# Attention into a feed-forward layer on one core: global heads on other PSUM banks, and a written order of three engines from step 18

## Chip, cores and metric

The kernel runs on one core of one Trainium2 chip. The time is in device microseconds of one execution. The profile is of one execution, taken on the chip.

## What is computed

The reference is cut to what matters. There are 8 batches of 8 heads, with 512 local and 32 global positions of width 64.

```python
k_all, v_all = concat([k_g, k_l], 2), concat([v_g, v_l], 2)
out_g = sm(scale * q_g @ k_all.T) @ v_all              # global queries see all
s_ll = where(abs(pos - pos.T) <= 32, scale * q_l @ k_l.T, -1e9)
out_l = sm(concat([scale * q_l @ k_g.T, s_ll])) @ v_all  # local: a window and the globals
x = concat([out_g, out_l], 2).transpose(0, 2, 1, 3).reshape(4352, 512)
h = relu(x @ w_in)                                     # 512 -> 2048
out = (s * h * h + b) @ w_out                          # 2048 -> 512
```

## The kernel before

**Steps.** One main loop runs over steps j. In steps 0 to 127 a step takes one head of one half of a batch (16 steps a batch: two halves of eight heads; batch b has steps 16b to 16b + 15). Steps 0 to 15 take heads in pairs. From step 10 on, each step also takes one eighth of a feed-forward tile of 256 tokens: with m = j − 10 (`LAG` is 10), `ffn_in(m)` makes 256 columns of the hidden layer, and `ffn_out(m − 1)` adds the part before to the output. There are 17 such tiles; the last holds the global rows.

**What a step does.** `scores(j)` has four matmuls into `ps_s` (L351), and between the first and the second of a block the product of the global queries with the same keys into `ps_g` (L363). DVE adds the mask and takes the minimum (L207), ACT exponentiates (L214), DVE normalizes (L223) and packs (L384), and a DMA transpose turns the weights (L386). One step later ACT copies them back (`join`, L394), and in odd steps `pv` multiplies a pair of heads with the values into `ps_op` (L318), which ACT copies into x (L325). The global product is read by ACT into `tg` (L371) and by DVE into `sg` (L372). `ffn_in` has 24 matmuls into `ps_h` (L493); ACT makes r (L501), DVE squares it (L502), ACT makes g (L509) and DVE its rest (L510). `ffn_out` has 12 matmuls into `acc` (L528). Numbers are split into a high and a low part of the type fp32r, so x is split as well (`x_split`, L464 on ACT and L465 on DVE, into `xs`), in steps 17, 25, 33 and so on. The split of the keys and queries (`kq`) runs on ACT (L191, L193) and on POOL (L192, L194).

**Global heads.** The rows `sg` of four heads fill up over a batch. Their softmax runs in steps 16b + 12 and 16b + 16 (`g_softmax`). Three steps later (16b + 15 and 16b + 19) `g_transposes` turns them on TensorE into a tile of blocks 0 to 3 and a tile of block 4 (both `ps_tg`, L417), ahead of the first and of the second half of `ffn_out`. ACT (L421) and DVE (L422) read each into `pg`. One and three steps after that `g_pv` multiplies `pg` with the split values `vsg` (L434 on ACT, L435 on POOL) into `ps_og` (L443), behind `ffn_in`. ACT (L447) and DVE (L448) read it, and a DMA stores the row.

**Banks.** The matmul results lie in eight PSUM banks, by tag: "s" (`ps_s`), "g", "t", "o", two of "h" (`ps_h`), "acc0" and "acc1". A tile of a tag waits until the tile before it in that bank has been read. "g" holds `ps_g`, `ps_og` and one tile of `ps_tg`; "t" holds the other tile of `ps_tg` and, up to step 15, the transposes of the first heads (`ps_t`); "o" holds `ps_op`.

**Order.** Up to step `ORDERED` the instructions of every engine are placed by a scheduler that weighs them by a model. From `ORDERED` on, TensorE, ACT and DVE take theirs in the order in which the program writes them; the queues of POOL and SP stay with the scheduler. In the step `ORDERED` itself the global product is made late, behind `ffn_in` (`late_scores`). All engines take their instructions strictly in order.

Of the kernel before, what the change touches and what calls it, by code (L numbers as in the profile page):

```python
# [10 lines left out]
F32 = mybir.dt.float32  # L11
# [10 lines left out]
P = 128  # L22
# [22 lines left out]
NF = 16  # L45
AHEAD = 0
LAG = 10
ORDERED = 25
WARM_FIRST = 28

SPARE = 12
# [11 lines left out]
def f32(ap):  # L63
    return ap.bitcast(F32)
# [3 lines left out]
def window_attention_then_ffn(ctx: ExitStack, tc: tile.TileContext, qd, qp, qg, kw, vw, vg, w_in, w_out, sv, bv, out):  # L68
# [5 lines left out]
    ps = ctx.enter_context(tc.tile_pool(name="ps", bufs=1, space=bass.MemoryType.PSUM))  # L74
# [266 lines left out]
    def scores(j):  # L341
        b, hf, h = slot(j)
        ks, qs = st_.pop(("ks", j)), st_.pop(("qs", j))
        p_s = ps.tile([P, 512], F32, tag="s", name=f"ps_s{j}")
        late = j == ORDERED
        if not late:
# [63 lines left out]
    def g_transposes(b, g):  # L410
        sg = st_["sg", b, g]
        pg = st_["pg", b, g] = sb.tile([P, 5, 4, 2, SG], F32R, tag="pg", name=f"pg{b}_{g}", bufs=1)
        for c0, c1, tag in ((0, 4, "g"), (4, 5, "t")) if b else ((4, 5, "g"), (0, 4, "t")):
            p_t = ps.tile([P, 4, P], F32, tag=tag, name=f"ps_tg{b}_{g}_{c0}")
            for c in range(c0, c1):
                s0 = min(c * P, SGW - P)
                nc.tensor.transpose(out=p_t[:, c - c0, :], in_=sg[:, s0:s0 + P], identity=ident)  # L417
            v = p_t[:, 0:c1 - c0].rearrange("p c (h q) -> p (c h) q", h=4)
            ph, pl = (pg[:, c0:c1, :, i, :].rearrange("p c h q -> p (c h) q") for i in range(2))
            with tc.high_priority():  # L420
                nc.scalar.copy(out=ph, in_=v)  # L421
                nc.vector.tensor_sub(out=pl, in0=v, in1=f32(ph))  # L422
            yield
# [13 lines left out]

    def g_pv(b, h):
        pg, vs = st_["pg", b, h // 4], st_.pop(("vsg", b, h))
        p_g = ps.tile([P, 512], F32, tag="g", name=f"ps_og{b}_{h}")  # L440
        for i in range(2):
            for c in range(5):
                nc.tensor.matmul(  # L443
                    p_g[0:64, i * P:(i + 1) * P], lhsT=pg[:, c, h % 4 + i], rhs=vs[:, i, c], start=(c == 0), stop=(c == 4),
                )
        t = sb.tile([32, 2 * P + 40], F32, tag="og", name=f"og{b}_{h}", bufs=1)[:, 0:2 * P]
        nc.scalar.copy(out=t, in_=p_g[32:64, 0:2 * P])  # L447
        nc.vector.tensor_add(out=t, in0=p_g[0:32, 0:2 * P], in1=t)  # L448
        xr = sb.tile([P, 264], F32, tag="xr", name=f"xr{b}_{h}", bufs=1)[0:32, 0:2 * D]
        t = t.rearrange("q (h a d) -> q h a d", h=2, a=2)  # L450
        nc.vector.tensor_add(out=xr.rearrange("q (h d) -> q h d", h=2), in0=t[:, :, 0], in1=t[:, :, 1])
        nc.sync.dma_start(xg_d[b * SG:(b + 1) * SG, h * D:(h + 2) * D], xr)
# [98 lines left out]
    for b in range(B):  # L551
        for g in range(2):
            s0 = 16 * b + G_AT[g]
            early[s0].append(lambda b=b, g=g: g_softmax(b, g))
            turns[s0 + G_TR] = g_transposes(b, g)
            for i in range(2):
                h = 4 * g + 2 * i
                early[s0 + G_TR + G_LD[i] - 1].append(lambda b=b, h=h: g_load(b, h))
                early[s0 + G_TR + G_LD[i]].append(lambda b=b, h=h: g_split(b, h))
                extra[s0 + G_TR + G_PV[i]].append(lambda b=b, h=h: g_pv(b, h))  # L560
# [21 lines left out]
    for j in range(NM + LAG + 2):  # L582
        if j == ORDERED:
            fixed.enter_context(tc.manual_schedule(engines=ENGINES))
# [32 lines left out]
        if 0 <= m < NM:  # L617
            t = m // 8 + 1
# [90 lines left out]
```

## Time and profile before

| | |
|---|---|
| median of 3 runs | 1042.64 us (1041.49 to 1045.37) |
| the profiled execution's own time | 1042.14 us |
| its span, first to last instruction | 1040.3 us |
| mean granted TensorE clock | 0.977 |
| TensorE matmul busy | 977.0 us (94%) |
| ScalarE (ACT) busy | 748.3 us (72%) |
| VectorE (DVE) busy | 691.8 us (66%) |
| GpSimd (POOL) busy | 273.1 us (26%) |

Busy time is the time in which an engine had an instruction running. A wait is the idle time of an engine ahead of an instruction, with the instruction on another engine that ended it. In a row of the timeline the first number is the start in us from the span's start, the second the duration, and what stands in square brackets is the wait; rows of equal instructions that follow each other are merged (x24). PE is TensorE, PEld its loading of weights.

### The profile page before, as it was taken

How to read it: one execution, taken by the hardware profiler on the slowest of the kernel's cores; microseconds unless marked ns; L12 is line 12 of the kernel's file. 1: busy time of each engine (PE TensorE's matmuls, PEld its weight loads, DVE VectorE, ACT ScalarE, POOL GpSimd, SP SyncE). 2: the span in 40 equal slices, each digit the busy share in tenths (PEclk: the TensorE clock that was granted, in tenths of full speed). 3: DMA queues.
4: the chain of work that ended last, by engine and by line, in shares of the span. 5: the costliest groups of instructions: out<-in, count | busy, mean ns of one | idle time of the engine just before them, and what ended most of it. 6: DMA issues, size and time to landing. Idle time of an engine off the chain costs nothing. (4 is left out here: it accounts for less than half of the span.)

```text
span 1040.3 us, 19938 instructions
## 1 busy us (share of the span) xinstructions
PE 977.0 (94%) x7060; PEld 862.5 (83%) x7060; DVE 691.8 (66%) x2092; ACT 748.3 (72%) x1618; POOL 273.1 (26%) x309
## 2 busy tenths in 40 slices
PE   5789998998999999998999999998999899999996
PEld 2468887887999889987999789987999789999895
DVE  6999667676667766776667766776667766653321
ACT  6987677778777777778778787777777787763221
POOL 0011322234323332234223342233323242221000
PEclk8679999999999999999999999999999999999998
DMA  9951444444444454444444454444444553321000
GB/s 327 350 176 61 99 115 100 109 105 121 107 108 99 100 123 116 109 102 121 117 108 98 103 129 103 109 106 125 103 115 96 104 131 91 87 62 35 11 21 20
DMA packets 179627, 115.07 MB, mean 111 GB/s; under 512 B 124744, under 2 KB 166728, under 8 KB 179528
## 3 DMA queue, kind: packets, MB, share of 16 engines
q1 hardware_dynamic: 179240, 112.76, 41.7%
q8 instruction: 55, 0.90, 0.4%
q10 hardware_dynamic: 288, 1.05, 0.4%
q14 instruction: 44, 0.36, 0.1%
HBM read 74.97 MB, written 9.44 MB: 81 GB/s over the span
## 5 line engine op out<-in xcount | busy, mean ns | idle before, releaser
L493 PE MATMUL ps_h<-xs,w 128*128 128x256 f32 x3264 | 421.1, 284 | 5.7 <-ACT xs L464 3.3
L493 PEld LDWEIGHTS ps_h<-xs,w 128*128 128x128 f32 x3264 | 399.0, 190 | 15.9 <-ACT xs L464 3.5
L528 PE MATMUL acc<-w,g 128*128 128x512 f32 x1632 | 404.2, 395 | 0.3 <-ACT g L509 0.2
L528 PEld LDWEIGHTS acc<-w,g 128*128 128x128 f32 x1632 | 294.8, 188 | 59.2 <-DVE g L510 1.1
L192 POOL TENSOR_TENSOR kq<-rk,kq 64x416 fp32r<-64x416 f32 x112 | 124.8, 1114 | 585.4 <-ACT kq L191 585.3
L509 ACT ACTIVATE g<-r,b_t 128x512 fp32r<-128x512 f32 x136 | 98.4, 724 | 123.0 <-DVE r L502 123.0
L510 DVE SCALAR_TENSOR_TENSOR g<-r,b_t,g 128x512 fp32r<-128x512 f32 x136 | 102.3, 752 | 99.8 <-ACT g L509 99.8
L394 ACT COPY ptp<-turned 128x1024 int16<-128x1024 int16 x112 | 152.7, 1363 | 6.2 <-DMA turned<-two 6.2
L502 DVE SCALAR_TENSOR_TENSOR r<-ps_h,s_t,r 128x512 f32<-128x512 f32 x136 | 101.3, 745 | 72.3 <-ACT r L501 70.6
L214 ACT ACTIVATE sm<-sm,nm 128x224 f32<-128x224 f32 (+1 forms) x256 | 117.8, 461 | 13.7 <-DVE nm L207 10.5
L501 ACT ACTIVATE r<-ps_h 128x512 f32<-128x512 f32 x136 | 81.4, 599 | 52.3 <-PE ps_h L493 49.5
L384 DVE COPY two<-sm 128x256 int16<-128x256 int16 x448 | 106.3, 300 | 0.1
L194 POOL TENSOR_TENSOR kq<-rq,kq 128x256 fp32r<-128x256 f32 x112 | 84.1, 751 | 8.8
L207 DVE CUSTOM_DVE_ANT_0 sm<-ps_s,mask 128x192 f32<-128x192 f32 (+1 forms) x224 | 74.4, 370 | 17.1 <-PE ps_s L351 16.8
L435 POOL TENSOR_TENSOR vsg<-rvg,vsg 128x320 fp32r<-128x320 f32 x64 | 55.7, 891 | 88.4 <-ACT vsg L434 88.4
L351 PE MATMUL ps_s<-kq 128*128 128x192 f32 (+1 forms) x448 | 78.7, 267 | 0.0
L351 PEld LDWEIGHTS ps_s<-kq 128*128 128x128 f32 x448 | 72.2, 191 | 7.4 <-issue 0.3
L223 DVE TENSOR_SCALAR sm<-sm,ss 128x192 f32<-128x192 f32 (+1 forms) x224 | 66.2, 337 | 3.9
L318 PE MATMUL ps_op<-ptp,rvp 128*64 128x128 f32 (+2 forms) x1024 | 67.8, 267 | 0.7 <-ACT ptp L310 0.6
L217 DVE TENSOR_SCALAR ss<-ss 128x2 f32<-128x2 f32 (+1 forms) x120 | 32.8, 273 | 51.4 <-ACT sm L214 51.2
L318 PEld LDWEIGHTS ps_op<-ptp,rvp 128*64 128x64 f32 x1024 | 53.6, 140 | 13.0 <-issue 2.7
L372 DVE TENSOR_TENSOR sg<-ps_g,tg 32x256 f32<-32x256 f32 (+1 forms) x112 | 48.2, 431 | 21.7 <-ACT tg L371 18.1
(68 smaller groups left out, 806.0 us busy)
## 6 DMA issues: line engine op xcount, KB each, us to landing
rvp<-in_vw SPq DMA_DIRECT2D x64, 256.0 KB, 2.8
rq<-in_qd SPq DMA_DIRECT2D x112, 128.0 KB, 2.3
rk<-in_kw SPq DMA_DIRECT2D x56, 208.0 KB, 2.5
rvg<-in_vg SPq DMA_DIRECT2D x32, 320.0 KB, 3.0
out<-o SPq DMA_DIRECT2D x34, 256.0 KB, 3.1
wst<-in_w_in SPq DMA_DIRECT2D x15, 512.0 KB, 6.3
wst<-in_w_out SPq DMA_DIRECT2D x15, 512.0 KB, 7.2
turned<-two SPq DMA_TRANSPOSE x112, 3.1
```

The costliest lines, as they stand in the source:

```text
L192: (nc.gpsimd if K_POOL(j) else nc.vector).tensor_sub(out=ks[p1:p1 + 64], in0=rk[p0:p0 + 64], in1=f32(ks[p0:p0 + 64]))
L194: nc.gpsimd.tensor_sub(out=qs[:, 1, :], in0=rq, in1=f32(qs[:, 0, :]))
L214: nc.scalar.activation(out=p, in_=p, func=AF.Exp, bias=nm[:, n:n + 1], scale=-1.0, accum_out=ss[:, n:n + 1],)
L318: nc.tensor.matmul(p_o[64 * k:64 * k + 64, 0, blk, q0:q0 + n], lhsT=rv[:, k, v:v + D], rhs=pt[:, k, o] if i < NF // 2 else pt[:, k, 2 * bl ...
L351: nc.tensor.matmul(p_s[:, cols], lhsT=qs[:, a, blk * P:(blk + 1) * P], rhs=ks[:, cols], start=(a == 0), stop=(a == 1),)
L384: nc.vector.tensor_copy(out=two[:, 2 * blk + c], in_=sm[:, :, c0:c0 + P])
L394: nc.scalar.copy(out=pt.bitcast(I16).rearrange("p c (q h) -> p c h q", h=2), in_=st_.pop(("turned", j)))
L493: nc.tensor.matmul(p_h[:, k], lhsT=wi[f][:, a, c, :], rhs=xs[:, e, c, :], start=(n == 0), stop=(n == 11),)
L502: nc.vector.scalar_tensor_tensor(out=r, in0=p_h, scalar=s_t, in1=r, op0=ALU.mult, op1=ALU.mult)
L509: nc.scalar.activation(out=g[:, 0], in_=r, func=AF.Identity, bias=b_t)
L510: nc.vector.scalar_tensor_tensor(out=g[:, 1], in0=r, scalar=b_t, in1=f32(g[:, 0]), op0=ALU.add, op1=ALU.subtract,)
L528: nc.tensor.matmul(oacc[t][i], lhsT=g[:, a, k, i * P:(i + 1) * P], rhs=wo[f][:, e, :], start=(pr == 0 and n == 0), stop=(pr == 7 and n == 5),)
```

## The change

The two tiles of `ps_tg` go to "t" (blocks 0 to 3) and "o" (block 4) in every batch, `ps_og` goes to "t", and the written order begins at step 18. "g" is left to `ps_g`.

```diff
-ORDERED = 25
+ORDERED = 18
...
     def g_transposes(b, g):
...
-        for c0, c1, tag in ((0, 4, "g"), (4, 5, "t")) if b else ((4, 5, "g"), (0, 4, "t")):
+        for c0, c1, tag in ((0, 4, "t"), (4, 5, "o")):
             p_t = ps.tile([P, 4, P], F32, tag=tag, name=f"ps_tg{b}_{g}_{c0}")
...
     def g_pv(b, h):
...
-        p_g = ps.tile([P, 512], F32, tag="g", name=f"ps_og{b}_{h}")
+        p_g = ps.tile([P, 512], F32, tag="t", name=f"ps_og{b}_{h}")
```

From step 27 on TensorE, ACT and DVE have the same instructions in the same order in both kernels; there only the banks differ. Steps 18 to 26 change their order, and the steps before them in places.

TensorE from the scores of step 18 on, before (the number behind a name is the step, the part of the feed-forward layer or the batch and head; the number at its end only tells buffers apart):

```order
L351 MATMUL ps_s18_1278<-kq18_1177 128x192 x2
L351 MATMUL ps_s18_1278<-kq18_1177 128x224 x2
L493 MATMUL ps_h8_1309<-xs1_1244,w0_152 128x256
L318 MATMUL ps_op8_1410<-ptp8_1212,rvp8_1066 64x128
L417 MATMUL ps_tg0_1_0_1472<-ident_66,sg4_335 128x128 x4
L493 MATMUL ps_h8_1309<-xs1_1244,w0_152 128x256 x11
L363 MATMUL ps_g17_1185<-kq17_1057,qgs1_981 64x256
L493 MATMUL ps_h8_1309<-xs1_1244,w1_195 128x256 x12
L528 MATMUL acc0_0_686<-w14_805,g7_1252 128x512 x3
L528 MATMUL acc0_0_686<-w15_817,g7_1252 128x512 x3
```

The same place with the change:

```order
L351 MATMUL ps_s18_1280<-kq18_1177 128x192 x2
L351 MATMUL ps_s18_1280<-kq18_1177 128x224 x2
L493 MATMUL ps_h8_1306<-xs1_1244,w0_152 128x256 x12
L493 MATMUL ps_h8_1306<-xs1_1244,w1_195 128x256 x12
L443 MATMUL ps_og0_2_1331<-vsg0_2_1214,pg0_0_1033 64x128 x10
L363 MATMUL ps_g18_1354<-kq18_1177,qgs1_981 64x256
L528 MATMUL acc0_0_686<-w14_805,g7_1252 128x512 x3
L528 MATMUL acc0_0_686<-w15_817,g7_1252 128x512 x3
L528 MATMUL acc0_1_687<-w14_805,g7_1252 128x512 x3
```

The transposes of the second four heads, a piece of `ps_op` and the global product of step 17 stood inside `ffn_in(8)` and have left it; the product of step 18 is the late one now, and `ps_og` of heads 2 and 3 stands ahead of it.

ACT from the exponentials of step 18 on, before:

```order
L214 ACTIVATE sm18_1287,ss18_1286<-sm18_1287,nm18_1285 128x192
L214 ACTIVATE sm18_1287,ss18_1286<-sm18_1287,nm18_1285 128x224
L371 COPY tg17_1196<-ps_g17_1185 32x256
L191 CAST kq20_1375<-rk20_1272 64x416
L193 CAST kq20_1375<-rq20_1274 128x256
L501 ACTIVATE r8_1351<-ps_h8_1309 128x512
L536 COPY o0_0_1369<-acc0_0_686 128x512
L509 ACTIVATE g8_1354<-r8_1351,b_t_72 128x512
L394 COPY ptp9_1421<-turned18_1304 128x4x2x128
L371 COPY tg18_1290<-ps_g18_1279 32x256
L191 CAST kq21_1485<-rk20_1272 64x416
L536 COPY o0_1_1372<-acc0_1_687 128x512
```

With the change:

```order
L214 ACTIVATE sm18_1287,ss18_1286<-sm18_1287,nm18_1285 128x192
L214 ACTIVATE sm18_1287,ss18_1286<-sm18_1287,nm18_1285 128x224
L394 COPY ptp8_1212<-turned17_1210 128x4x2x128
L447 COPY og0_2_1342<-ps_og0_2_1331 32x256
L501 ACTIVATE r8_1348<-ps_h8_1306 128x512
L509 ACTIVATE g8_1351<-r8_1348,b_t_72 128x512
L371 COPY tg18_1356<-ps_g18_1354 32x256
L536 COPY o0_0_1371<-acc0_0_686 128x512
L536 COPY o0_1_1374<-acc0_1_687 128x512
L191 CAST kq20_1377<-rk20_1274 64x416
L193 CAST kq20_1377<-rq20_1276 128x256
L371 COPY tg19_1396<-ps_g19_1385 32x256
```

The casts of the keys and queries of steps 20 and 21 stood between r, g and the stores of `acc` and now follow them; the copy of `ps_og` and r and g of part 8 have moved ahead of them.

## Rows read from the trace of the kernel before

**Rows 1.** Page, part 1: busy time of each engine, share of the span, instructions.

```profile
PE 977.0 (94%) x7060; PEld 862.5 (83%) x7060; DVE 691.8 (66%) x2092; ACT 748.3 (72%) x1618; POOL 273.1 (26%) x309
```

**Rows 2.** Who TensorE waits for, whole span: total us, times, longest us.

```profile
PE ps_g L363 <- DVE pg L422: 20.2, 12, 2.2
PE ps_og L443 <- DVE sg L372: 7.0, 7, 1.1
...
PE ps_h L493 <- DVE xs L465: 1.7, 6, 0.3
```

**Rows 3.** Windows from one step's first `ps_s` to the next: steps 48, 50-54, 60.

```profile
core 0: us, PE busy (x) PEld busy (x) DVE busy (x) ACT busy (x) POOL busy (x), PEclk, DMA share, GB/s
...
342.27:350.37 8.10, 6.93 (x53) 6.22 (x51) 5.95 (x22) 5.80 (x14) 1.81 (x2) 1.00 0.49 117
357.71:366.18 8.47, 7.23 (x52) 6.35 (x51) 7.03 (x20) 5.59 (x13) 2.28 (x3) 1.00 0.43 110
366.18:373.93 7.75, 7.75 (x64) 6.93 (x62) 4.30 (x16) 6.62 (x15) 3.13 (x4) 1.00 0.56 159
373.93:383.11 9.18, 6.99 (x52) 6.23 (x51) 5.90 (x21) 6.71 (x15) 2.20 (x3) 1.00 0.57 131
383.11:390.26 7.15, 7.15 (x59) 6.43 (x58) 4.76 (x16) 6.08 (x14) 3.60 (x4) 1.00 0.57 76
390.26:397.03 6.77, 6.77 (x52) 6.25 (x51) 4.60 (x18) 4.98 (x12) 1.81 (x2) 1.00 0.61 159
430.77:436.89 6.12, 6.12 (x42) 5.63 (x41) 4.38 (x16) 4.53 (x10) 1.83 (x2) 1.00 0.45 104
```

**Rows 4.** Timeline, steps 48 to 50: start us, us, engine, line [idle before, releaser].

```profile
342.85 0.88 DVE L422 TENSOR_TENSOR pg<-ps_tg,pg 128x512 fp32r<-128x512 f32 x2
...
343.68 0.30 PE L363 MATMUL ps_g<-kq,qgs 128*64 128x256 f32 x1 [1.17 <-DVE pg L422]
...
344.35 0.36 DVE L207 CUSTOM_DVE_ANT_0 sm<-ps_s,mask 128x192 f32<-128x192 f32 x1 [0.62 <-PE ps_s L351]
...
351.59 0.72 ACT L509 ACTIVATE g<-r,b_t 128x512 fp32r<-128x512 f32 x1 [1.43 <-DVE r L502]
...
357.31 2.04 DVE L465 TENSOR_TENSOR xs<-x,xs 128x512 fp32r<-128x512 f32 x2 [0.81 <-ACT xs L464]
...
358.80 1.44 PE L493 MATMUL ps_h<-xs,w 128*128 128x256 f32 x10 [0.26 <-DVE xs L465]
```

**Rows 5.** Timeline, steps 50 and 51: the second wait, and the copy of `ps_op`.

```profile
362.18 0.42 DVE L372 TENSOR_TENSOR sg<-ps_g,tg 32x256 f32<-32x256 f32 x1
...
362.74 0.79 PE L443 MATMUL ps_og<-vsg,pg 128*64 128x128 f32 x10 [0.97 <-DVE sg L372]
...
370.57 0.37 ACT L325 COPY x<-ps_op 128x256 f32<-128x256 f32 x1
...
372.43 0.27 PE L417 MATMUL ps_tg<-ident,sg 128*128 128x128 f32 x1
```

**Rows 6.** Timeline, step 52: the third wait, and `ps_og` behind it.

```profile
375.63 0.88 DVE L422 TENSOR_TENSOR pg<-ps_tg,pg 128x512 fp32r<-128x512 f32 x2
...
376.37 0.33 PE L363 MATMUL ps_g<-kq,qgs 128*64 128x256 f32 x1 [2.19 <-DVE pg L422]
...
379.69 0.76 PE L443 MATMUL ps_og<-vsg,pg 128*64 128x128 f32 x10
```

**Rows 7.** Windows of steps 36 and 100, columns as in rows 3.

```profile
256.62:267.38 10.76, 8.56 (x52) 7.78 (x51) 5.93 (x21) 6.69 (x15) 2.20 (x3) 0.84 0.49 114
721.14:731.76 10.62, 8.40 (x53) 7.68 (x52) 5.91 (x21) 6.70 (x15) 2.18 (x3) 0.84 0.51 115
```

**Rows 8.** Steps 18 to 25: their window, the late `ps_g`, and the page's turns.

```profile
119.73:184.50 64.77, 59.61 (x430) 51.50 (x429) 44.74 (x133) 45.30 (x100) 18.97 (x20) 1.00 0.40 100
...
181.56 0.34 PE L363 MATMUL ps_g<-kq,qgs 128*64 128x288 f32 x1 [2.44 <-DVE sg L372]
...
turned<-two SPq DMA_TRANSPOSE x112, 3.1
```

## The prediction

> **What bounds the kernel now.** I first read the page's busy times: TensorE is busy for 977.0 us [rows 1], so of the 1040.3 us span at most some 63 us can be won by closing its gaps. Next I read who TensorE waits for over the whole span [rows 2]. One name leads: the product of the global queries, `ps_g` (L363), waits 20.2 us in 12 places for DVE's `pg` (L422), and `ps_og` (L443) waits 7.0 us in 7 places for `sg` (L372). Neither pair shares data. What they share is the bank "g": the next user waits until the last one has been read out. Third, I cut one batch (steps 48 to 63, j of the main loop) at the start of each step's first `ps_s` matmul [rows 3]. Step 54 is even, holds one `ps_og`, and takes 6.77 us. Steps 48, 50 and 52 hold the same work and take 8.10, 8.47 and 9.18 us. They lose 1.33, 1.70 and 2.41 us, 5.44 us a batch, and six batches (steps 32 to 127) run so. The reader should see that TensorE is busy throughout the other steps, so a closed gap is worth its full length unless another wait opens behind it.
>
> Last, the timeline around the three places, which I call the first, second and third wait.
>
> First wait, step 48 [rows 4]: `ps_g` stands 1.17 us until DVE has read the transposes. DVE ends L422 at 342.85 + 0.88 = 343.73 and then itself waits for `ps_s`, until 344.35. From there a long DVE and ACT chain runs (softmax of the global heads, then r, then the split of x). In it ACT waits 1.43 us for DVE, not for TensorE. It ends in `xs` (L465), for which TensorE waits at 358.80, in step 50.
>
> Second wait, step 50 [rows 5]: `ps_og` stands 0.97 us for L372, which ends at 362.18 + 0.42 = 362.60.
>
> Third wait, step 52 [rows 6]: `ps_g` stands 2.19 us for L422, which ends at 375.63 + 0.88 = 376.51.
>
> **The change, part by part.** *Banks.* "t" is free from step 16 on, and "o" holds `ps_op` in odd steps alone. No instruction is added or removed, so each wait falls to whatever is late next.
>
> The first wait mostly moves. Without it `ps_s` is ready when DVE ends L422, and the chain starts at 343.73 in place of 344.35: 0.62 us earlier, no more, since the rest of the chain does not hang on TensorE. `xs` is ready 0.62 us earlier and TensorE waits for it in step 50 all the longer. The bounds are 0 (another part of the chain binds) and 1.33; the row nearest is the 0.62 us gap of DVE, and I take 0.6.
>
> The second wait goes. `ps_og` no longer needs L372; next is g, which `acc` needs behind it. ACT's part of that chain is 0.6 us earlier too, and `acc` starts only after `ps_og`. Bounds 0 and 1.70; I take the wait itself, 1.0, since the rest of the 1.70 is the wait for `xs`.
>
> The third wait goes. TensorE comes to step 52 about 1.6 us earlier (372.3 for 373.93). Then `ps_g` runs at once, and the next that needs `pg` is `ps_og` in the same step, 379.69 − 376.37 = 3.3 us behind `ps_g` [rows 6], so at about 375.9. L422 now ends at 376.51 − 0.6 = 375.9. That is a tie; a wait of a few tenths is possible. Bounds: 0.6, if this wait also only moves, and 2.41. The next split of x comes in step 57, and ACT is busy 6.08 us of 7.15 in step 53, 4.98 of 6.77 in step 54 and 4.53 of 6.12 in step 60 [rows 3], so the chain can catch up before it. I take 2.4.
>
> Who is behind the moved tiles? The last transpose (`ps_tg`, columns of block 4) now waits in "o" for the copy of `ps_op` (L325). That copy ends at 370.57 + 0.37 = 370.94 and the transpose starts at 372.43 [rows 5]. With TensorE 1.6 and ACT 0.6 us earlier, 370.8 against 370.3: 0.5 us of margin, so nothing, with the gain's own size as the other bound (a rival below).
>
> Six batches: 6 × (0.6 + 1.0 + 2.4) = 24.0 us.
>
> *Clock.* In two of the six third waits the granted clock falls: steps 36 and 100 show a mean of 0.84 and take 10.76 and 10.62 us, against 9.18 in step 52 at 1.00 [rows 3, 7]. TensorE had just stood idle for 2.2 us. The two cost 1.58 + 1.44 = 3.0 us. The wait left in step 50, about 0.8 us, is far shorter, so I take 3.0; the bounds are 0 and 3.0. The Trainium skill ("TensorE: Matmul & The Clock Gate", section on psum-queue depth-cycling) says that small idles between groups, as banks cycle, make the clock swing between its two levels. The trace agrees in two of six places; by that rule the wait left in step 50 could cost a dip as well, and the 3.0 would be a swap.
>
> *Start of the written order.* Steps 18 to 25 take 64.77 us now [rows 8]. By written steps with no wait they need 3 × 6.77 (18, 20, 22, with `ps_og`) + 7.75 (19, with the transposes) + 3 × 7.15 (21, 23, 25) + 6.12 (24) = 55.6 us [rows 3]. So 9.1 us are lost, 2.44 of it in one place: the late `ps_g` of step 25 waits for L372 of the one before [rows 8]. Written out, each product follows its own scores and ACT no longer serves several heads' pieces in turn. What stays: the wait for `xs` in step 18 (step 50 shows its kind; about 1.0), the late product, which now sits in step 18 and keeps `ps_g` of step 19 waiting (between 0 and the 2.44 of the present one; 0.7, since only one product is late and `acc` covers 3 us behind it), and `vsg`, which ACT now casts only after r and g of the step (0.6). I take 9.1 − 2.3 = 6.8, bounds −1 and 9.1.
>
> DMA queues: SP and POOL are still placed by the scheduler. On SP, two loads now stand ahead of the transpose of head 16, and each batch's load of values changes places with a row store. A turn takes 3.1 us from issue to landing [rows 8] and is used a step later, so I cost this at nothing; if a load held the queue for long, `ptp` would be late by that much, once. POOL casts head 19 ahead of `vsg`; both are needed a step later.
>
> Sum: 24.0 + 3.0 + 6.8 = 33.8 us off the profiled execution's own 1042.1, **1008.3 us**. That execution is 0.5 us under the median of the three runs shown (1042.64), so I say **1008.5**.
>
> **The rivals.**
>
> *All of it comes back.* ACT is busy 72% of the span and DVE 66% [rows 1]; if that idle time can be used, the chain of step 48 follows TensorE, each batch returns its whole 5.44 us, and the start its 9.1: 1042.1 − 6 × 5.44 − 3.0 − 9.1 = 997.4. Against it: inside that chain ACT stands 1.43 us for DVE [rows 4], idle time that nothing can fill. The Trainium skill ("Perfetto Trace Analysis", section on identifying the most-contended engine) takes occupancy as a fair measure for ScalarE and VectorE, and by it this rival would be the forecast; the wait in the chain speaks against the rule here. Chance 0.08.
>
> *The third wait only moves*, as the first does: `ps_og` of step 52 then waits for `pg`. For it: the tie at 375.9. It gives back 6 × 1.8 = 10.8, so 1019. Chance 0.14.
>
> *The start wins nothing*: the written order meets ACT and DVE still busy with the last weights. 1042.1 − 27.0 = 1015. Chance 0.06.
>
> *The bank was not the limit*: the chain of DVE and ACT is as long as the step, and every wait comes back under another name. About 1040. Against it: TensorE waits for `xs` only 1.7 us in the whole span [rows 2]. Chance 0.04.
>
> *Slower, through bank "o".* At the 14 turns that have scores behind them the last transpose stands in the middle of `acc`, so a late copy L325 stops TensorE there, and everything queued behind it: half of `acc`, then the next scores. For the sum to turn by over 5.2 us, each of the 14 waits must exceed (33.8 + 5.2) / 14 = 2.8 us, so L325 must come 3.3 us later than I have it. At 3.2 us a wait it is 1042.1 − 33.8 + 14 × 3.2 = 1053. Against it: L325 is ready 1.5 us ahead today [rows 5]. Chance 0.04.
>
> **How the numbers follow.** The forecast has 0.64. A measurement of this kernel can tell some 0.5%, 5.2 us, from no change. Faster by more: 0.64 + 0.08 + 0.14 + 0.06 = 0.92; the same 0.04; slower 0.04. The range starts at 1000, between the forecast and the case where all returns, which it leaves out, and reaches to 1021, which takes in the third wait moved (1019) or the start unchanged (1015), not both (1026).
>
> **What would show it.** Right: no `ps_g` waits for L422 and no `ps_og` for L372; step 52 takes about 6.8 us and step 48 too, while step 50 stays near 8.2 with a wait for L465 of about 0.8 us; no dip of the clock after step 32; steps 18 to 25 take about 58 us. Wrong: waits of `ps_og` for L422 near 2 us in steps 52, of `ps_tg` for L325, or of `acc` for g.

## The result, and the profile after

The changed kernel takes 1009.55 us (median of 4 runs, 1008.9 to 1010.45), the kernel before 1042.62 (1041.49 to 1045.37): a ratio of 0.968, interval 0.9659 to 0.97. The forecast was 1008.5, in the range 1000 to 1021. The profiled execution of after took 1010.45 us itself, with a span of 1008.0; that of before had a span of 1040.3, so 32.3 us of span are gone.

The page's busy times, after:

```profile
PE 969.8 (96%) x7060; PEld 861.2 (85%) x7060; DVE 688.1 (68%) x2092; ACT 744.2 (74%) x1618; POOL 274.7 (27%) x309
```

The counts are those of [rows 1]: nothing was added or left out, the gaps of TensorE closed. Cut step by step, the granted clock of after is 1.00 in every step from 18 to 127, where before it fell in steps 36 and 100 [rows 7].

Who TensorE waits for over the whole span, after (total us, times, longest us):

```profile
PE ps_h L493 <- DVE xs L465: 6.0, 9, 1.1
...
PE ps_og L443 <- DVE pg L422: 1.6, 6, 0.4
...
PE ps_g L363 <- DVE sg L372: 1.4, 1, 1.4
```

Both leading names of [rows 2] are gone (`ps_g` for `pg`, 20.2 us; `ps_og` for `sg`, 7.0). Three small waits stand in their place. `xs` has grown from 1.7 us to 6.0.

Windows of after, cut as in [rows 3]: steps 18 to 25, 18 to 31, then steps 36, 48, 50, 51, 52 and 100 (us, then busy us of PE, PEld, DVE, ACT, POOL; behind them the clock, the DMA share and GB/s):

```profile
120.75:177.98 57.23, 55.79 (x429) 50.56 (x427) 39.63 (x132) 44.84 (x98) 18.53 (x20) 1.00 0.49 113
120.75:218.41 97.66, 96.22 (x727) 87.35 (x726) 67.87 (x228) 77.73 (x170) 32.09 (x35) 1.00 0.47 111
248.39:255.55 7.16, 6.95 (x52) 6.26 (x51) 5.14 (x18) 6.24 (x15) 3.40 (x4) 1.00 0.53 131
330.39:337.13 6.74, 6.74 (x53) 6.25 (x51) 5.23 (x19) 5.13 (x13) 1.83 (x2) 1.00 0.46 123
344.29:352.49 8.20, 7.54 (x52) 6.45 (x51) 6.11 (x17) 6.41 (x15) 3.94 (x4) 1.00 0.43 109
352.49:360.23 7.74, 7.74 (x64) 6.89 (x63) 5.08 (x18) 6.11 (x15) 1.81 (x3) 1.00 0.62 160
360.23:367.51 7.28, 6.93 (x52) 6.26 (x51) 5.13 (x18) 6.36 (x15) 3.53 (x4) 1.00 0.51 128
696.18:703.40 7.22, 6.95 (x53) 6.26 (x51) 5.14 (x18) 6.30 (x15) 3.47 (x4) 1.00 0.51 123
```

In steps 48 and 51 TensorE is busy from end to end. Step 50 keeps 0.66 us of idle time and step 52 0.35.

Timeline of after at the three places of [rows 4 to 6], and in step 19:

```profile
129.16 0.33 PE L363 MATMUL ps_g<-kq,qgs 128*64 128x256 f32 x1 [1.44 <-DVE sg L372]
...
330.48 0.28 PE L363 MATMUL ps_g<-kq,qgs 128*64 128x256 f32 x1
...
331.06 0.88 DVE L422 TENSOR_TENSOR pg<-ps_tg,pg 128x512 fp32r<-128x512 f32 x2
...
331.86 0.35 DVE L207 CUSTOM_DVE_ANT_0 sm<-ps_s,mask 128x192 f32<-128x192 f32 x1
...
339.25 0.72 ACT L509 ACTIVATE g<-r,b_t 128x512 fp32r<-128x512 f32 x1 [1.45 <-DVE r L502]
...
344.97 1.98 DVE L465 TENSOR_TENSOR xs<-x,xs 128x512 fp32r<-128x512 f32 x2 [0.82 <-ACT xs L464]
...
345.72 0.97 PE L493 MATMUL ps_h<-xs,w 128*128 128x256 f32 x6 [0.34 <-DVE xs L465]
...
347.00 2.25 PE L493 MATMUL ps_h<-xs,w 128*128 128x256 f32 x17 [0.31 <-DVE xs L465]
...
349.09 0.76 PE L443 MATMUL ps_og<-vsg,pg 128*64 128x128 f32 x10
...
358.20 0.38 ACT L325 COPY x<-ps_op 128x256 f32<-128x256 f32 x1
...
358.63 0.14 PEld L417 LDWEIGHTS ps_tg<-ident,sg 128*128 128x128 f32 x1 [0.17 <-ACT x L325]
...
363.26 0.88 DVE L422 TENSOR_TENSOR pg<-ps_tg,pg 128x512 fp32r<-128x512 f32 x2
...
364.09 0.78 PE L443 MATMUL ps_og<-vsg,pg 128*64 128x128 f32 x10 [0.35 <-DVE pg L422]
```

Read it from the top. In step 19 the product behind the late one waits 1.44 us. `ps_g` of step 48 starts at once, though L422 has yet to read the transposes. L207 follows L422 without a wait, and the chain behind it still stands 1.45 us at L509. `xs` is late in step 50 (0.34 + 0.31 us). `ps_og` of step 50 no longer waits, and in step 52 it waits 0.35 us for `pg`. The weights of the last transpose wait 0.17 us for L325, the matmul itself not at all.

### The profile page after: what moved, and what is told of

Its sections match the earlier page's. It is cut to its first block, busy times and chain, and to the rows that moved or that the text cites. A ratio compares the mean times of both kernels' runs of the same rounds, so it can differ in the third digit from the quotient of the medians.

```text
span 1008.0 us, 19973 instructions
## 1 busy us (share of the span) xinstructions
PE 969.8 (96%) x7060; PEld 861.2 (85%) x7060; DVE 688.1 (68%) x2092; ACT 744.2 (74%) x1618; POOL 274.7 (27%) x309
## 4 chain that ended last, share of the span: by engine, by line
PE 48%; ACT 17%; DVE 10%; issue 2%; DVEq 0%; ACTq 0%
PE acc L528 21%; PE ps_h L493 20%; ACT sm L214 3%; DVE r L502 3%; PE ps_op L318 3%; ACT ptp L394 3%; ACT g L509 3%; PE ps_s L351 2%; ACT kq L191 2%; DVE two L384 1%; DVE xs L465 1%; ACT kq L193 1%; ACT tg L371 1%; PE ps_og L443 1%; ACT vsg L434 1%
## 5 line engine op out<-in xcount | busy, mean ns | idle before, releaser
L509 ACT ACTIVATE g<-r,b_t 128x512 fp32r<-128x512 f32 x136 | 98.4, 724 | 126.5 <-DVE r L502 126.5
L510 DVE SCALAR_TENSOR_TENSOR g<-r,b_t,g 128x512 fp32r<-128x512 f32 x136 | 102.1, 751 | 102.9 <-ACT g L509 102.9
L384 DVE COPY two<-sm 128x256 int16<-128x256 int16 x448 | 100.5, 287 | 0.0
L207 DVE CUSTOM_DVE_ANT_0 sm<-ps_s,mask 128x192 f32<-128x192 f32 (+1 forms) x224 | 74.2, 368 | 7.0 <-PE ps_s L351 6.8
L217 DVE TENSOR_SCALAR ss<-ss 128x2 f32<-128x2 f32 (+1 forms) x120 | 37.4, 312 | 45.6 <-ACT sm L214 45.5
L372 DVE TENSOR_TENSOR sg<-ps_g,tg 32x256 f32<-32x256 f32 (+1 forms) x112 | 48.2, 431 | 20.7 <-ACT tg L371 17.3
```

Source lines behind the costliest of these rows:

```text
L384: nc.vector.tensor_copy(out=two[:, 2 * blk + c], in_=sm[:, :, c0:c0 + P])
L509: nc.scalar.activation(out=g[:, 0], in_=r, func=AF.Identity, bias=b_t)
L510: nc.vector.scalar_tensor_tensor(out=g[:, 1], in0=r, scalar=b_t, in1=f32(g[:, 0]), op0=ALU.add, op1=ALU.subtract,)
```

## The experiments

My theory was the prediction's: TensorE was held by a shared bank, and removing all holds on one chain lets the whole loop follow. The rivals were that one bank alone was the cause, that the start and not the batches won the time, and that the wait had only taken another name. Ratios are to the kernel before, run beside each experiment on the same chip. Its median was 1042.62 to 1043.63 us in the four sets of runs, so a difference of about 1 us between two experiments of different sets says nothing by itself.

**The banks alone.** The change, with the written order from step 25 as before.

```diff
-ORDERED = 18
+ORDERED = 25
```

> The banks alone: tiles as in the changed kernel, written order from step 25 as before. Theory (each wait goes to what is late next): the six batches from step 32 on take 112.0 us each as in the changed kernel, some 25 us in all less than before, with no dip of the clock; of the 64.8 us of steps 18 to 25 the two waits of bank g go (2.0 us), the 2.4 us of the late product stay. About 1015.5 us. Rival (the order from step 18 on sets the pace of the batches, the banks are side matter): 1035 or more.

Measured: 1021.43 us, ratio 0.9791 (0.9773 to 0.9808), 5.9 above the theory. The batches came out as in the change: 111.3 to 112.0 us each, where before has 115.6 to 117.1. But the start is worse than before. Step 32 begins at 230.83 us, before at 225.67, after at 218.41. The window and the timeline of step 26, the costliest there; the last row is the product of step 26 before:

```profile
183.18:196.54 13.36, 8.92 (x42) 8.24 (x41) 7.81 (x24) 8.32 (x17) 1.79 (x2) 0.74 0.29 65
...
180.26 0.30 PE L363 MATMUL ps_g<-kq,qgs 128*64 128x288 f32 x1
...
186.80 0.39 ACT L371 COPY tg<-ps_g 32x288 f32<-32x288 f32 x1
...
188.09 0.50 PE L363 MATMUL ps_g<-kq,qgs 128*64 128x288 f32 x1 [4.44 <-DVE sg L372]
...
188.55 5.37 PE L493 MATMUL ps_h<-xs,w 128*128 128x256 f32 x24
```

```profile
185.44 0.35 PE L363 MATMUL ps_g<-kq,qgs 128*64 128x288 f32 x1 [0.47 <-DVE sg L372]
```

Before, the late product of step 25 itself waits 2.44 us [rows 8], and the one behind it 0.47. Here the late product (180.26) waits for nothing, but ACT reads it only at 186.80, behind the split of x and r and g of the same step, and the product of step 26 waits 4.44 us. The clock falls there (a mean of 0.74 over the step), and the 24 matmuls of `ps_h` take 5.37 us, against 2.98 for the 24 of step 48 with the change. So the gain in the batches belongs to the banks, and the banks alone spoil the start. This last I had not expected.

**The order alone.** The banks of before, with `ORDERED = 18`.

> The order alone: written from step 18, banks as before. Theory: the batches from step 32 on stay at 115.6 to 117 us with all three waits; steps 18 to 25 take about 61 us, since the late product now stands right behind ps_og in bank g and waits for its copy, and step 20 gets the third wait. About 1038.5 us. Rival (the two parts add up, the order's share is 33 less 27): 1036 or less, with steps 18 to 25 near 57 us.

Measured: 1036.46 us, ratio 0.9944 (0.9921 to 0.9967). Steps 18 to 25 take 60.87 us, against 64.77 before and 57.23 after: the theory's 61, not the rival's 57, although the median lies near the rival's total. The five runs spread from 1034.63 to 1040.39 us, and the profiled one is the slowest; the clock falls in three of its third waits, in two before. Waits of TensorE over the whole span, then step 18:

```profile
PE ps_g L363 <- DVE pg L422: 21.2, 13, 2.2
PE ps_og L443 <- DVE sg L372: 8.0, 7, 1.8
```

```profile
125.81 0.78 PE L443 MATMUL ps_og<-vsg,pg 128*64 128x128 f32 x10 [1.76 <-DVE sg L372]
...
127.49 0.33 PE L363 MATMUL ps_g<-kq,qgs 128*64 128x256 f32 x1 [0.90 <-DVE og L448]
```

All the batches' waits are still there. In the shared bank "g" the first written step has three users in a row (a `ps_g`, `ps_og`, the late product), and each waits for the reader of the one before. Behind these two waits the clock falls too (a mean of 0.85 over step 18, which takes 11.49 us).

**One bank at a time.** First `ps_og` alone to "t", the rest as before:

```diff
     def g_pv(b, h):
-        p_g = ps.tile([P, 512], F32, tag="g", name=f"ps_og{b}_{h}")
+        p_g = ps.tile([P, 512], F32, tag="t", name=f"ps_og{b}_{h}")
```

> Of the banks only ps_og moves to t; transposes stay in g and t, order from step 25. Theory: the second wait (1.0 us) goes, but ps_g of step 52 still stands until L422, which does not come earlier, so the third wait grows from 2.2 to 3.2 us and the batch stays at 115.6: 1041.5 us, within 0.3% of before. Rival (each wait is worth its length by itself): 6 x 1.0 and the first batch's, 1036 us.

Measured: 1044.3 us (median of 10), ratio 1.0016 (1.0001 to 1.003): no gain. Waits over the whole span, then the windows of steps 51 and 52:

```profile
PE ps_g L363 <- DVE pg L422: 23.1, 12, 3.5
...
PE ps_tg L417 <- DVE sg L372: 3.6, 6, 0.7
```

```profile
364.17:372.73 8.56, 7.96 (x63) 6.95 (x62) 4.97 (x18) 6.29 (x15) 2.72 (x4) 1.00 0.55 149
372.73:383.17 10.44, 6.98 (x52) 6.24 (x51) 6.38 (x21) 7.29 (x16) 2.60 (x3) 1.00 0.51 118
```

The second wait is gone, and all of it comes back. The transposes, still in "g", now wait for L372 in step 51, and step 52 takes 10.44 us where before took 9.18 (9.55 to 11.12 in the other batches). The batches from steps 64 and 80, in which the clock stays up, take 115.7 and 115.8 us, as before. The third wait grew to 2.6 us in five batches and to 3.46 in this one, against 3.2 in the theory.

Then the transposes alone, to "t" and "o", with `ps_og` left in "g":

```diff
-        for c0, c1, tag in ((0, 4, "g"), (4, 5, "t")) if b else ((4, 5, "g"), (0, 4, "t")):
+        for c0, c1, tag in ((0, 4, "t"), (4, 5, "o")):
```

> Of the banks only the transposes move to t and o; ps_og stays in g, order from step 25. Theory: the first wait moves to xs (0.6 us won), the third goes but ps_og of step 52 then waits about 0.5 us for L372 of the same step, the second (1.0 us) stays: 6 x (0.6 + 2.4 - 0.5) and 3 us of the clock, 1024.5 us. Rival (parts add up: 27 us of the banks less 6 x 1.0): 1021.5 us; rival (ps_og in g is the root of all three): 1038 or more.

Measured: 1028.09 us, ratio 0.9856 (0.9837 to 0.9875). Batches take 113.0 to 113.1 us, about 2.6 less than the batches of before without a dip of the clock, as forecast (2.5). The start is worse, as with all banks moved (step 32 at 232.08 us), and that was not forecast. Waits over the whole span, and the window of step 49:

```profile
PE ps_og L443 <- DVE sg L372: 6.8, 9, 1.1
PE ps_g L363 <- DVE og L448: 5.4, 7, 1.1
```

```profile
351.20:359.44 8.24, 7.39 (x58) 6.44 (x57) 6.05 (x20) 6.73 (x17) 3.14 (x4) 1.00 0.27 69
```

Step 49 has lengthened from 7.34 us (357.71 − 350.37, [rows 3]) to 8.24: `ps_og` of step 48, no longer held up by a wait ahead of it, keeps `ps_g` of step 49 waiting until it is read. Apart, the two parts win −0.7 and 15.5 us (of 1043.57 for the kernel before, run beside them), and together 22.1.

**The tiles exchanged.** The change, with the large tile in "o" and the small one in "t":

```diff
-        for c0, c1, tag in ((0, 4, "t"), (4, 5, "o")):
+        for c0, c1, tag in ((0, 4, "o"), (4, 5, "t")):
```

> The changed kernel with the two tiles of the transposes exchanged: blocks 0 to 3 in o, block 4 in t. The tile in o now comes half an ffn_out (1.8 us) earlier, at 356.9 in step 51, and the copy L325 that frees o ends at about 358.5. Theory (bank o decides where the copy comes after the transposes): TensorE waits for L325 some 1.6 us in each step 51 and loses, with the tie of step 52 given back, 1.3 us a batch: about 1018 us. Rival (the margin is larger than the rows say, or the chain takes the wait up): 1011 us or less.

Measured: 1016.9 us, ratio 0.9755 (0.9731 to 0.9778). The wait over the whole span, and the windows of steps 51 and 52:

```profile
PE ps_tg L417 <- ACT x L325: 9.0, 6, 1.6
```

```profile
352.94:362.44 9.50, 7.96 (x63) 6.95 (x62) 5.78 (x19) 7.04 (x17) 3.50 (x4) 1.00 0.57 148
362.44:369.21 6.77, 6.77 (x53) 6.26 (x51) 5.56 (x19) 5.51 (x14) 1.82 (x2) 1.00 0.52 123
```

This is what the rival through bank "o" described. The transposes that come first in `ffn_out` meet the copy of `ps_op` too early and stop TensorE 1.5 us in step 51; the tie of step 52 then has room. It shows that the copy L325 does decide, and that placing the small, later tile in "o" keeps just clear of it.

**The late product taken out.** The change, with the product of step 18 made beside its scores:

```diff
-        late = j == ORDERED
+        late = False
```

> The changed kernel without the late product: the global product of step 18 stands among its scores as in every other step. Theory (the late product costs its wait of 1.44 us and the refill in step 19, 9.40 for 7.75 us): 1008 us, step 19 near 7.8. Rival (the wait moves into step 18, where the product then waits for the sum of step 17): within 0.5 us of the changed kernel, 1009.5, or above it.

Measured: 1007.58 us, ratio 0.9666 (0.9645 to 0.9687), 2.0 below the change. The intervals of the two ratios overlap; the traces tell them apart. Steps 18 to 31, and step 19:

```profile
120.92:216.97 96.05, 96.05 (x728) 87.41 (x726) 67.36 (x228) 77.06 (x170) 31.65 (x35) 1.00 0.45 113
127.67:135.41 7.74, 7.74 (x63) 6.93 (x62) 4.53 (x15) 6.47 (x15) 3.54 (x4) 1.00 0.58 160
```

Step 19 loses its 1.44 us wait, and TensorE is then busy without a gap through all 14 steps, which take 96.05 us in place of 97.66. Steps 18 to 25 take 55.61 us, the 55.6 that the prediction had added up for written steps with no wait.

**The same with the banks alone.** Banks of the change, `ORDERED = 25`, `late = False`. This asks why the banks alone spoil the start.

> The banks of the change, the written order still from step 25, and no late product in step 25 (its two halves of products stay together). Theory (what the banks lose at the start is the late product alone: 4.4 us of wait and a stretch at half clock behind it): about 1013.5 us, step 26 at 9 to 10 us rather than 13.4, and no clock below 0.9 after it. Rival (the scheduler's own order in steps 18 to 24 is what the banks do not suit; the wait moves into another step): 1019 us or more.

Measured: 1017.82 us, ratio 0.9758 (0.9729 to 0.9787), between theory and rival. Windows of steps 18 to 31, of step 26 and of step 23; then who TensorE waits for from step 18 to step 25:

```profile
120.49:224.49 104.00, 99.91 (x727) 87.75 (x726) 71.32 (x228) 75.72 (x166) 30.99 (x34) 1.00 0.43 102
182.49:189.82 7.33, 6.66 (x43) 5.74 (x41) 5.57 (x19) 6.23 (x13) 1.84 (x2) 1.00 0.28 59
...
158.48:167.26 8.78, 7.95 (x59) 6.40 (x57) 5.58 (x18) 5.29 (x12) 1.81 (x2) 1.00 0.35 82
```

```profile
PE acc L528 <- ACT g L509: 2.0, 2, 1.3
PE acc L528 <- DVE g L510: 1.1, 1, 1.1
```

Both theories hold in part. Step 26 fell from 13.36 to 7.33 us and the clock stays up, so the late product of step 25 did cost that; in the runs it is worth 1021.43 − 1017.82 = 3.6 us, since some returns later (the batch from step 32 takes 113.3 us for 111.3). But steps 18 to 31 still take 104.00 us. The kernel to compare with is the change without the late product: there they take 96.05, and it is 1017.82 − 1007.58 = 10.2 us faster. So most of what the written order wins given the banks lies in the scheduler's own placing of steps 18 to 24. `acc` waits for g in steps 21, 23 and 24, which take 8.58, 8.78 and 8.05 us, where the written order takes 7.15, 7.17 and 6.10. These three steps make 5.0 of the 6.4 us by which steps 18 to 25 are longer (62.00 against 55.61), though the profile shows only 3.1 us of waits in them: step 23 has 7.95 us of busy time for the same 59 matmuls that take 7.17 written. A step's length tells more here than the waits shown. The other 1.4 us lie in steps 18 and 19; what makes them stays open.

**The chain behind step 48 reordered.** The change, with the softmax of the global heads cut in two. Its maximum stays in place; the exponential and the rest follow `ffn_in`, behind r and g of the step:

```diff
         nc.vector.tensor_scalar_mul(gm, gm, -scale)
+        yield
         nc.scalar.activation(out=v, in_=v, func=AF.Exp, bias=gm, scale=scale, accum_out=gs)
...
-            early[s0].append(lambda b=b, g=g: g_softmax(b, g))
+            softmaxes[s0] = g_softmax(b, g)
...
+        rest = softmaxes.pop(j, iter(()))
+        next(rest, None)
         for fn in early.pop(j, []):
...
             ffn_in(m, then)
+            list(rest)
...
```

> The changed kernel, with the softmax of the global heads cut in two: its maximum stays where it is, its exponential and the rest are written behind ffn_in, after r and g, so that ACT no longer stands 1.5 us for gm in step 48. Theory (what is left of the first wait is the length of the chain of ACT and DVE up to xs): the chain gets about 2 us shorter, the wait for xs goes, step 50 falls from 8.2-8.3 to about 6.8 us, and the batch from 112.0 to 110.5; the tie at pg in step 52 stays. About 1001 us. Rival (the split of x itself, its 1.2 us on ACT and 2 us on DVE, is what TensorE waits for): step 50 stays above 8 us, 1008 us or more.

Measured: 999.67 us, ratio 0.9589 (0.9567 to 0.961), 9.9 below the change. Windows of steps 50, 52 and 100:

```profile
342.33:349.10 6.77, 6.77 (x52) 6.27 (x51) 5.36 (x18) 4.98 (x11) 1.82 (x2) 1.00 0.47 118
356.82:364.71 7.89, 6.94 (x52) 6.26 (x51) 5.14 (x18) 6.27 (x15) 3.33 (x4) 1.00 0.49 119
688.38:695.43 7.05, 6.94 (x53) 6.26 (x51) 5.15 (x18) 6.13 (x15) 3.28 (x4) 1.00 0.54 131
```

ACT in step 48: the exponential (L405) before and with the change, then g with the softmax cut in two (L510 there, since the lines have moved by one):

```profile
348.43 0.75 ACT L405 ACTIVATE sg<-sg,gm 128x544 f32<-128x544 f32 x1 [1.40 <-DVE gm L404]
```

```profile
336.09 0.75 ACT L405 ACTIVATE sg<-sg,gm 128x544 f32<-128x544 f32 x1 [1.54 <-DVE gm L404]
```

```profile
334.70 0.72 ACT L510 ACTIVATE g<-r,b_t 128x512 fp32r<-128x512 f32 x1 [1.13 <-DVE r L503]
```

ACT no longer stands for the maximum (gm), since the exponential now runs behind g; its wait ahead of g stays, 1.13 us for 1.45. The split of x on DVE starts 12.86 us behind the start of step 48, where the change has 14.58, so the chain is 1.7 us shorter. Step 50 has no wait left, and that is worth 8.20 − 6.77 = 1.43 us, although the change showed only 0.66 us of idle time in it: the rest stood as busy time of the same 52 matmuls. The tie at `pg` stays, once with 0.95 us (step 52), otherwise with a tenth or so (step 100).

**Both together.** This last cut and `late = False` on top of the change.

> The softmax cut in two and no late product, both on top of the changed kernel. If the two are independent, their gains add up: about 999.5 us. If the start hides the one behind the other: that of the softmax alone, 1001.

Measured: 998.11 us (996.79 to 999.14), ratio 0.9572 (0.955 to 0.9594), the lowest median of all. The two gains measured apart, 9.9 and 2.0 us, would give 997.7, so they add up. The interval overlaps that of the softmax alone (1.6 us slower); in the traces steps 18 to 25 take 55.6 us here and 57.2 there. TensorE is busy 965.0 us of its span of 995.5.

## Why the prediction was right

The sum was 33.8 us off 1042.1; the profiled executions show 32.3 us off the span. By its own steps:

- **First and second wait**, taken as 0.6 + 1.0 a batch. From the start of step 48 to that of step 51 before took 366.18 − 342.27 = 23.91 us, after 352.49 − 330.39 = 22.10: 1.81 won. "Mostly moves" holds. L207 starts 1.47 us into step 48 in place of 2.08, the 0.6 that the gap of DVE allowed, and L465 starts 14.58 us behind the start of step 48 in place of 15.04 and ends 16.56 in place of 17.08 [rows 4]: 0.5 us earlier, against 0.6 taken. Step 50 keeps 8.20 us. Its wait shows as 0.65 us, in four of the six batches as 1.06, against about 0.8 forecast; what it costs, 8.20 − 6.77 = 1.43 us, is what the sum had left of a batch (5.44 − 4.0). The 0.2 more than forecast is step 49, which ran 7.34 us before and is 7.16 now.
- **Third wait**, taken as 2.4: 9.18 − 7.28 = 1.90. The tie that I priced at nothing came out on the wrong side, in all six places, for up to 0.4 us. TensorE came to it 1.8 us earlier and not 1.6, and L422 ends only 0.5 us earlier (33.75 us behind the start of step 48, before 34.24) and not 0.6: together the 0.3 us of the wait. The rival in which this wait only moves (1.8 us) was wrong, though a quarter of it happened.
- **Clock**, taken as 3.0. Steps 36 and 100 win 3.60 and 3.40 us, 3.2 more than two times 1.90. The rule of the Trainium skill ("TensorE: Matmul & The Clock Gate", section on psum-queue depth-cycling), by which the wait left in step 50 could dip the clock too, did not hold for waits of this size: none of the waits in the batches of after, at most 1.1 us, shows one.
- **Start**, taken as 6.8: 64.77 − 57.23 = 7.54. The size came near, its parts were not right. I left a loss of 2.3 us for the late product (0.7), `xs` (1.0) and `vsg` (0.6). There is one wait only, the late product's 1.44 us, and with it taken out these steps need 55.61 us, so nothing else was lost in them. Step 18 itself starts 1.0 us later than before, which I had not costed.
- **Sum**: 6 × (1.81 + 1.90) + 3.2 + 7.54 − 1.0 = 32.0, against 32.3. Steps 26 to 31, for which I had no term, win 0.7 more (41.17 us before, 40.43 after), and the other batches win a little less than the one shown. So part of the closeness is luck: 3.0 us too much for the third waits and 1.0 for the later start of step 18 stand against 1.3 too little for the first two waits, 0.7 for steps 18 to 25 and 0.7 for steps 26 to 31.

Two things in the working hid behind the right total. My sum gave the batches to the banks and the start to the order. As stretches of the changed kernel they add up; as shares of two independent parts they do not: alone the parts win 22.1 us (1043.57 − 1021.43) and 7.1 (1043.57 − 1036.46), together 33.1 (1042.62 − 1009.55). The rival "the start wins nothing" had 1015 for the banks without a gain of the order; the banks alone came to 1021.43.

And the chain of step 48 was not as fixed as I took it. I named one idle time of ACT in it, 1.43 us ahead of L509, which "nothing can fill", and overlooked a second of the same size ahead of the exponential (L405, for gm): 1.40 us before, 1.54 with the change. The experiment that moves the exponential behind r and g does away with the second; of the first 1.13 us stay. It reaches 999.67, near the 997.4 of the rival in which everything comes back. As the forecast for this change that rival stays wrong: both waits are there.

The margin at the copy of `ps_op` was sized at 0.5 us and was about nothing (the wait of 0.17 us on the weights). It held, and the exchanged tiles show that 1.5 us less of it would have cost 7.4 us over six batches.

## What to carry to other kernels

When several waits hang on one shared buffer along one chain, cost them together: taking one away can be worth nothing (`ps_og` alone: ratio 1.0016) because the next wait grows by as much, while all of them together are worth 22 us. For each wait that is to go, find the time at which its successor's operand is ready and treat a tie as a loss of a few tenths. Idle time of an engine inside a chain is a property of the order on that engine; look for work that could change places with the waiting instruction before calling it fixed.

## What was not expected

The length of a wait alone does not tell whether the clock falls. With only `ps_og` moved, `ps_g` waits 2.60 us in step 36 and 3.46 us in step 52:

```profile
258.27 0.33 PE L363 MATMUL ps_g<-kq,qgs 128*64 128x256 f32 x1 [2.60 <-DVE pg L422]
...
376.44 0.33 PE L363 MATMUL ps_g<-kq,qgs 128*64 128x256 f32 x1 [3.46 <-DVE pg L422]
```

The shorter one is followed by a dip (step 36: mean clock 0.85, 11.13 us), the longer one is not (step 52: 1.00, 10.44 us). Before shows the same with waits of one length: two dips in six. What else decides stays open. And a product made late has no fixed price. Before, it waits 2.44 us itself and the product behind it 0.47; with the banks alone it does not wait and the one behind it does, 4.44 us; with the change the one behind it waits 1.44.
